# A two-layer transformer prompt kernel: another order of its TensorE products

## The chip, the cores and the metric

The kernel runs on one core of a Trainium2 chip, in one launch. The metric is device microseconds of one execution; of several executions the median is given.

## The reference, cut to what matters

The input is 2048 rows of 576 (one batch). Two blocks are applied twice, with the same weights both times: a block A with residual on its layer norm, and a block B with residual on its layer norm.

```
def _A_ref(x, mem0, Wq, Wk, Wv, Wo, seg_len):      # seg_len 32, 64 segments
    mem = mem0                                      # 8 rows
    for s in range(n_seg):
        h = concat([mem, x[segment s]])             # 40 rows
        q, k, v = h Wq, h Wk, h Wv                  # 32 heads of 128
        p = softmax(mask(q k^T * scale))
        o = (p v) Wo
        mem = o[:, :8]; outs.append(o[:, 8:])
...
x = x + A(layernorm(x)); x = x + B(layernorm(x))
x = x + A(layernorm(x)); x = x + B(layernorm(x))
```

B is a gated FFN, `silu(x w1) * (x w3)` times w2, with 4608 hidden columns. A is recurrent: a segment needs the 8 memory rows that the segment before it put out.

## The kernel before, in words

Work is done in steps t. Step t runs segment t of the first layer and segment t - 8 of the second (LAG 8) side by side: 80 columns where both layers have a segment, 40 where one has. There are 64 + 8 = 72 steps. Every four steps 128 rows of a layer are complete and go through the FFN as a "job"; the FFN weights come from DRAM in 18 pairs of 256 hidden columns for every job, through two buffers for w1 and w3 (tile W13, in the profile W from in_B_w_dram) and two for w2 (W2C). All matmul results go to eight PSUM banks.

The program is a graph of nodes (`make_nodes`): each is a small bundle of instructions on one engine with its cost, the nodes it depends on, and the buffers it takes and gives back. `plan` walks the graph and puts out the order in which the nodes are recorded; each engine then executes its own instructions in that order. For VectorE (DVE), ScalarE (ACT), GpSimd (POOL) and the load queue (SP), `plan` picks the ready node that can start first. For TensorE (PE) the order is fixed beforehand: a string, one letter for each product, `ORDER = FIRST + FOUR * 11 + LAST`. FIRST has 805 letters, FOUR 224 (four steps and their FFN job), LAST 684. The letters that the text uses:

| letter | product | matmuls |
|---|---|---|
| Q, q | queries and keys of one unit of four heads (8 units a step), main part and the last 64 of 576 rows ("tail") | 32, 8 |
| S | scores of a group of 8 heads (4 groups a step) | 16 or 8 |
| T | transposes of the softmax result, written to tile PTS by ACT or DVE | 8 |
| P | T's result times V, copied to tile OT | 8 |
| O, o | OT times Wo, main part and tail | 32, 8 |
| V, v, X, x, G, g | values of the memory rows, of the x rows, or of both, and tails | 8 to 32 |
| F, f | FFN up for one weight pair, main part and tail | 16, 4 |
| W, w | FFN down for two weight pairs, first and second layer | 8 |
| p, n, a, b | transposes around residual and layer norms | 5 |

Between S and T stand seven or eight instructions on DVE and ACT: add of the mask, maximum, subtraction, exp, sum, reciprocal, and three or four multiplications into tile PB. Between F, f and W stand a tanh on ACT and two multiplications on DVE. The first Q of a step needs the memory columns that ACT and DVE write from the last o of the step before.

TensorE works in tile modes. Tails of q, f and g are in "row" mode (two matmuls of 64 rows side by side), o is in "col" mode (64 columns), Q and O are in "full" mode, the narrow V in "c32", "oct" or "quad". T, P, F, W, G, p and n may run in full or in col mode; `plan` lets them take the mode of their neighbours. In col mode `mm` (line 586) splits each matmul into two halves of 64 columns.

All loads of weights are on SP's queue, in the planned order. A load for a buffer waits for the product that reads the buffer's old content. For the last job the weights are not streamed through W13: once the last step has read Wq, Wk and Wv, their tiles W and WV are overwritten by four big loads (`tail_load`, 2.4 MB each for W and 1.2 MB for WV). Pairs 16 and 17 are loaded once for the two last jobs. Every matmul is recorded by line 591, every ACT instruction by 594, DVE 597, SP loads 600, ACT's loads 603.

In step 0 the first Q of units 0 and 4 puts 12 matmuls of 512 columns on the identity ahead of its own (`qk`), if its q has not come before. The X products of step 0 issue nothing of their own; the V of step 0 issues both.

Of the kernel before, what the change touches and what calls it, by code (L numbers as in the profile page):

```python
# [44 lines left out]
class Slot:  # L45


    def __init__(self, pool, users=1):
        self.pool, self.users, self.i, self.end, self.begun = pool, users, None, 0.0, False
# [144 lines left out]
def ewh(*ns):  # L194
# [2 lines left out]


FIRST = (
    "amQQQQqqqqSSqqQQQTSQqqSxXVvPTPTOPOOTooPoOoQQqqqvSVqQQQSqQqqQSTxqPQTSOPXoTOPTaPOOoooQQqqqqQSQQSQqqqVSTvQQqXPTSPTO"  # L200
    "POOToooPOoxQQqqqQSVqvQQqSqQTQPSqqQOTSoPOTPTOPooOoQQpqqqQvSVQnqQFSqfqQQTSfqqFPQFTSOfoPWTOFPfTOPFOoooWQqqfQQSQFfqq"
    "vVfSFTWQFqqfQPQFSqqfQTXPSWTFOfPOTxOPFOooooWQQqqqfQSFqfqVvQWTQSFfqPQQSfqqFTQOSfPFTOaFPWTOPooofOoFQqqfQQSWqqfQFSvV"
    "TQqqQWPQSQTPOqqOboSoTXPXTPOOooxxQQpQqqqVqQnvSSFqfQqQFfQTSfqqFPQTOPSWTFFPffOTOPWOooooFQQqfqqQQqfSWFGSqqgQTQFPQgqf"
    "SGTFqfQOoSPWFfggGTGPOaTWPOOoooFQQvqfqVSFqqfQQQqqfSFQTQFqfqSQWPFfSTOPFTWPOffooOTFPWOooFQqfqqQQWSQQqQqSqqbQSTGggqQ"
    "PGTOSPGTggOPGTOPoooOoQqqqpQpQQqvVSSnnQFqfqqQQTFPqffSQOTWPFOSTwFPffFTOWPwOooooFqqffQQFQqqwWSFqqfQQQwWSTSGqgfFPQFf"
    "qgTGQPGTfgSWFgPGTOOPOOwooooFqqfQQQWQffqqFwFSSVvFQfqqQQTQWqqSwPFaSTffFPOTOWPwfTFPOOooooWQQqqqqQSbQQQSqqGTQgqqSQPG"
    "TgggSGPGTOPOTOPwOoooo"
)
FOUR = (
    "QqqvpQQpQqqVSSnnQQFffqqFQTQqqfSFPwTWFSffOPFTWPOTOPwOooooFqfqqQQQWQqwSSFFffgqGQTQPQgqqqGTwSQPWGSFTfgfgFPGOTOPOwOo"  # L210
    "oooFqffqQFQWQqSVvQQQqqqfFTWPwSSFFqffqQQTOwSWPFTffFOPWTwPOOooooFqqfqQQQWQSqqqaQSQQbQgqqSGTSGPgTGPOTggGPOTOPwOoooo"
)
LAST = (
    "QqqqpQQpQSqqqQQnVvSnSQTFqfqfQPFTOFPoSTwFfPOTOPWOoooFqffqQQQQqqfSFWSGwqqgQQTQPFgqffFTGWwPFSgffqFQWGSwTFPGTgfOPOOO"
    "ooooWFqqfqQQQSwQqqqVSvQTQFPQqSfqfFTQWwPSOTFffPOTOPFOWoooowQQqfqFSQwQWFqqfVSTvWQQqqPQQqqSTOSoPVvwTOPbTOPooxOoXqqQ"
    "QpvQqqSVpQQqqQSTQPqqQSnnOFffToSFPTOPFTOPWOooowQfqfqFQQSvqqVQFSfqqQQwTSWPQFTffqqQOPSWTFPFTOwPOOooooXfqxFQQQqfqfqF"
    "SQwVvSWQFTQqqfqQWPQSTwqffFPOFSWTOPwFffTOPFOWooowoFqqfQQQSFQqfqvVSTQqqfQWwPSFTqqQPQWSTOPOOooowbTxPOoXqqQQQpSQqvqV"
    "qSnQQFffqFQqqSQTPSTFfPOwOToFPofTOPFOoowQfqqfQFSQVvqqqQQSFQfqqqQSQTwPSFTFPffXTOOPxTOPwOooooFQfqqVvQQQSqfqFSQQfqqq"
    "FQTSQPwqOTSFPofTFPOOTPwOoooQfqqqQQSwFQqfqvSVqTQQqPQSQqTSfOPFOTfooPFTOPOooFpwnfffFFwFwfffFFFwfffFFwFwfffFFFwfffFF"
    "wFwfffFFFfww"  # L220
)
ORDER = FIRST + FOUR * 11 + LAST
# [2 lines left out]
class Opt:  # L225

    qk, qkt, sc, tr, pv, wo, wog, vm = 0.0079, -0.0342, 0.0268, 0.1447, 0.0406, 0.2653, 0.0725, 0.1407
    vmt, vx, vxt, ff, fft, win, w2, gstep = -0.0231, 0.2313, 0.0843, 0.2124, -0.1839, 0.8 * (LAG - 4), 0.1943, 0.0624
    ustep, mode_pen, hor, wait, bulk, ff_split, last_win, tail_at = 0.0315, 0.1194, 0.0162, 0.141, 0.02, False, 2.5, -1.5

# [337 lines left out]
class Emitter:  # L568


    def __init__(self, nc, tc, T, aps, nseg):
        self.nc, self.tc, self.T, self.nseg = nc, tc, T, nseg
        self.a = aps
        self.last = {}
        self.order_dep = mybir.DependencyInfo(mybir.DependencyClass.NoSync, mybir.DependencyReason.SCHED_ONLY)
        self.tail_w, self.ys, self.mode = {}, {}, None


    def ch(self, eng, inst):
# [287 lines left out]
    def v_parts(self, strips, r):  # L867

        return [(p0, m, row, 2 * q + r) for p0, _, q, m, row in strips]

    def vx(self, t, k, b, tail):
        def f(n):
            if t == 0 and not tail:
                self.x0 = (b, self.vx_strips(t, k))
                return
            self.v_mm(t, [(b, self.vx_strips(t, k))], tail)
        return f

    def vm(self, t, k, b, tail):
        return lambda n: self.v_mm(t, ([self.x0] if t == 0 and not tail else []) + [(b, self.vm_strips(t, k))], tail)  # L880

    def v_ev(self, b, p0, width, row, blk):
        return lambda n: self.cp(n, self.T.V[row:row + width, blk, :], self.bk(b)[p0:p0 + width, :])
# [444 lines left out]
```

## Time and profile before

| | us |
|---|---|
| median of 4 runs | 2694.91 |
| lowest, highest | 2691.28, 2697.9 |
| the profiled execution | 2697.9 |
| its span | 2696.1 |
| PE busy in it | 2629.5 |
| DVE busy | 2103.5 |
| ACT busy | 1362.0 |

By the starts of the first matmuls in the trace, FIRST begins at 13.3 us and the first FOUR at 530.9; the eleven FOUR take 156.30 to 157.62 us each; LAST begins at 2255.3. A line of a group names the engine, the operation, out<-in with the shapes, the count, the busy time and the mean of one. A line of the timeline has start and length, and in brackets the idle time before and what ended it. "Issue" means that the profile shows nothing that the engine waited for. A busy time of PE is modelled from pipelined matmuls; the distance between starts is the safer measure.

### The profile page before, as it was taken

To read this page: it belongs to the slowest core of one execution; us is meant where nothing else is said; L and a number is where in the kernel's file an instruction comes from. 1 tells how busy PE (TensorE), PEld (TensorE's weight loads), DVE (VectorE), ACT (ScalarE), POOL (GpSimd) and SP (SyncE) were. 2 spreads that over 40 slices of the span, in tenths; PEclk is the share of its full clock that TensorE was granted. 3 is DMA by queue.
4 is the path that set the end of the run, shared out by engine and by line. 5 is a ranking of instruction groups with operands and counts; after the bars stand their busy time and mean duration, and the time that the engine had idled before them with its cause. 6 is when DMAs were issued, how large, how long until landed. Compare 5 with 4: busy or idle time off the path is not lost.

```text
span 2696.1 us, 137075 instructions
## 1 busy us (share of the span) xinstructions
PE 2629.5 (98%) x60995; PEld 2287.0 (85%) x60995; DVE 2103.5 (78%) x5463; ACT 1362.0 (51%) x3938; POOL 332.4 (12%) x400
## 2 busy tenths in 40 slices
PE   5999999999999999999999999999999999999998
PEld 4788888889888888888888888888888888888886
DVE  5777786887888788787878878787887878787776
ACT  2645554554545455454545545454545545454552
POOL 1111110110111011011101101010110101011110
PEclk8999999999999999999999999999999999999999
DMA  9064524343342334334233434424243442434457
GB/s 317 7 179 112 155 83 131 89 128 109 109 128 81 108 96 127 109 111 128 80 111 92 128 108 117 126 80 112 87 128 108 117 126 65 122 89 134 127 169 246
DMA packets 478178, 322.08 MB, mean 119 GB/s; under 512 B 26024, under 2 KB 467760, under 8 KB 476944
## 3 DMA queue, kind: packets, MB, share of 16 engines
q1 hardware_dynamic: 474048, 305.43, 38.6%
q8 instruction: 477, 7.82, 1.2%
q0 software_dynamic: 3024, 6.93, 0.9%
q10 hardware_dynamic: 512, 0.94, 0.1%
q14 instruction: 117, 0.96, 0.1%
HBM read 308.49 MB, written 2.36 MB: 115 GB/s over the span
## 4 chain that ended last, share of the span: by engine, by line
PE 85%; DVE 7%; DMA 3%; ACT 2%; issue 1%; SPq 1%; POOL 0%; ACTq 0%; DVEq 0%
PE bank L591 85%; DVE STAT L597 1%; DMA W<-in_B_w_dram 1%; SPq L600 1%; DVE SME L597 1%; ACT V L594 1%; DVE HTT L597 1%; DVE PB L597 1%; DMA W<-in_A_Wk_dram 1%; DVE V L597 1%; DVE XN L597 0%; DMA WO<-in_A_Wo_dram 0%; DVE LNS L597 0%; DMA XN<-in_A_x_dram 0%; DVE XR L597 0%
## 5 line engine op out<-in xcount | busy, mean ns | idle before, releaser
L591 PEld LDWEIGHTS <-W 128*128 128x128 bf16 (+2 forms) x32176 | 1268.2, 100 | 132.0 <-issue 64.2
L591 PE MATMUL bank<-HT,W 128*128 128x80 bf16 (+3 forms) x23040 | 812.0, 197 | 20.7 <-issue 9.6
L591 PE MATMUL bank<-XTB,W 128*64 128x256 bf16 (+5 forms) x9136 | 660.7, 263 | 7.2 <-DMA W<-in_B_w_dram 4.2
L594 ACT ACTIVATE QKT<-bank 128x64 bf16<-128x64 f32 (+2 forms) x1500 | 349.7, 312 | 352.5 <-PE bank L591 346.8
L1006 POOL MEMSET PB<- 128x1024 bf16 x288 | 274.1, 952 | 1832.4 <-PE bank L591 1553.8
L591 PE MATMUL bank<-OT,WO 128*128 128x80 bf16 (+3 forms) x11520 | 407.0, 198 | 3.3 <-ACT OT L594 1.3
L591 PEld LDWEIGHTS <-WO 128*128 128x128 bf16 (+1 forms) x11520 | 380.0, 102 | 20.7 <-issue 9.2
L594 ACT ACTIVATE V<-bank 64x512 bf16<-64x512 f32 (+1 forms) x606 | 343.0, 585 | 94.6 <-PE bank L591 85.9
L591 PE MATMUL bank<-WV,HT 128*32 128x512 bf16 (+5 forms) x3584 | 373.4, 382 | 1.1 <-DMA WV<-in_A_Wv_dram 0.7
L591 PE MATMUL bank<-W2C,HTT 128*64 128x288 bf16 (+1 forms) x3072 | 323.5, 287 | 0.4 <-DMA W2C<-in_B_w_dram 0.4
L594 ACT ACTIVATE HTT<-bank 128x512 bf16<-128x512 f32 (+1 forms) x324 | 176.6, 553 | 211.3 <-PE bank L591 210.3
L597 DVE TENSOR_REDUCE STAT<-SME 104x8 f32<-104x320 f32 (+1 forms) x576 | 274.2, 476 | 11.5 <-ACT SME L594 6.3
L597 DVE TENSOR_TENSOR PB<-SME,STAT 40x128 bf16<-40x128 f32 (+4 forms) x912 | 275.0, 336 | 8.5 <-DVE STAT L597 0.5
L597 DVE SCALAR_TENSOR_TENSOR XR<-bank,XR 128x288 f32<-128x288 f32 x576 | 245.9, 446 | 23.4 <-PE bank L591 19.2
L597 DVE SCALAR_TENSOR_TENSOR HTT<-HTT,bank 128x512 bf16<-128x512 bf16 (+1 forms) x324 | 201.8, 623 | 74.8 <-ACT HTT L594 70.5
L591 PEld LDWEIGHTS <-HT 128*32 128x32 bf16 (+5 forms) x3584 | 154.4, 98 | 124.5 <-issue 17.0
L591 PEld LDWEIGHTS <-HTT 128*64 128x64 bf16 (+1 forms) x3136 | 223.7, 105 | 34.5 <-issue 1.2
L594 ACT ACTIVATE OT<-bank 128x320 bf16<-128x320 f32 (+1 forms) x420 | 155.2, 403 | 148.9 <-PE bank L591 146.0
L597 DVE TENSOR_TENSOR HTT<-HTT,bank 128x512 bf16<-128x512 bf16 (+1 forms) x324 | 203.7, 629 | 27.8 <-DVE HTT L597 0.5
L594 ACT ACTIVATE SME<-SME 104x320 f32<-104x320 f32 (+1 forms) x288 | 135.3, 470 | 165.9 <-DVE SME L597 164.2
L597 DVE CAST QKT<-bank 128x128 bf16<-128x128 f32 (+4 forms) x548 | 147.6, 316 | 88.6 <-PE bank L591 86.4
L594 ACT ACTIVATE PTS<-bank 128x320 bf16<-128x320 f32 (+1 forms) x383 | 143.9, 403 | 131.8 <-PE bank L591 118.5
(61 smaller groups left out, 1832.6 us busy)
## 6 DMA issues: line engine op xcount, KB each, us to landing
W<-in_B_w_dram SPq DMA_DIRECT2D x612, 256.0 KB, 3.6
W2C<-in_B_w_dram SPq DMA_DIRECT2D x306, 288.0 KB, 3.3
W<-in_B_w_dram SPq DMA_DIRECT2D x612, 32.0 KB, 3.3
W<-in_B_w_dram SPq DMA_DIRECT2D x8, 1024.0 KB, 12.5
W<-in_A_Wq_dram SPq DMA_DIRECT2D x9, 512.0 KB, 9.1
WO<-in_A_Wo_dram SPq DMA_DIRECT2D x4, 1152.0 KB, 17.6
XR<-in_A_x_dram POOLq DMA_DIRECT2D x16, 288.0 KB, 3.7
WV<-in_B_w_dram SPq DMA_DIRECT2D x4, 1152.0 KB, 10.7
```

Of the source, the lines that this page charges most:

```text
L591: self.ch("PE", self.nc.tensor.matmul(out, lhsT=lhsT, rhs=rhs, start=start, stop=stop, skip_group_check=True, **k))
L594: self.ch("ACT", self.nc.scalar.activation(*a, **k))
L597: self.ch("DVE", getattr(self.nc.vector, fn_)(*a, **k))
L600: self.ch("SP", self.nc.sync.dma_start(out=out, in_=in_))
L1006: return lambda n: self.ch("POOL", self.nc.gpsimd.memset(self.T.PB[:, pb.i], 0.0))
```

## The change

The three strings get new contents of the same lengths (805, 224, 684) with the same letters in number. The last 52 letters of LAST, `oFpwnfff...`, are the same. No node, cost, pool or load of the graph is changed. `plan` runs on the new strings, so the orders of DVE, ACT, POOL and SP follow them.

A second edit lets the V and the X of step 0 stand in either order: the one that comes second issues the matmuls of both, where before it was always V.

```diff
 FIRST = (
-    "amQQQQqqqqSSqqQQQTSQqqSxXVvPTPTOPOOTooPoOoQQqqqvSVqQQQSqQqqQSTxqPQTSOPXoTOPTaPOOoooQQqqqqQSQQSQqqqVSTvQQqXPTSPTO"
+    "amqqQQQqSQqqQqSqqQSQTSvxVXPTPTOPTOPooOOooQQqqqqQSQvqqSVQqQTqSQPQOSToPXTOPTxoPOOooQqqqQQSVvqQQSQqqqSqTQPQOSTPTOP"
...
 FOUR = (
-    "QqqvpQQpQqqVSSnnQQFffqqFQTQqqfSFPwTWFSffOPFTWPOTOPwOooooFqfqqQQQWQqwSSFFffgqGQTQPQgqqqGTwSQPWGSFTfgfgFPGOTOPOwOo"
-    "oooFqffqQFQWQqSVvQQQqqqfFTWPwSSFFqffqQQTOwSWPFTffFOPWTwPOOooooFqqfqQQQWQSqqqaQSQQbQgqqSGTSGPgTGPOTggGPOTOPwOoooo"
+    "QvqqpQQpQqqVSSnnQQFqfqfFQTQfqqWSFPwTFPSfOOTFPwTOPWOooooFffqqQQQQqqSWFSFffqgGQTQPQQgqqqGSwTFPGSfgfgFTGOPOWTOPwOoo"
+    "ooFqqQQQQqfqVvSSwWFfqfqQQTFWQwQSFffqqFPWTOPSowTFPffOTOFPWwOoooFqqfqQQQWQSqqqaQSQQbQqgqSGTSGPgTGPOTggOPGTOPwOoooo"
 )
...
-    "FQTSQPwqOTSFPofTFPOOTPwOoooQfqqqQQSwFQqfqvSVqTQQqPQSQqTSfOPFOTfooPFTOPOooFpwnfffFFwFwfffFFFwfffFFwFwfffFFFwfffFF"
+    "QQPwqqFTSOfPFTOfPwTOPfoooOoFQQqqqqQSQQSqqQVvSfTFPqQQwqfTSFPOTOFPTOPfoooOoFpwnfffFFwFwfffFFFwfffFFwFwfffFFFwfffFF"
     "wFwfffFFFfww"
...
+    def v_run(self, t, b, strips, tail):
+
+        if t or tail:
+            self.v_mm(t, [(b, strips)], tail)
+            return
+        self.v0.append((b, strips))
+        if len(self.v0) == 2:
+            self.v_mm(t, self.v0, False)
+
     def vx(self, t, k, b, tail):
-        def f(n):
-            if t == 0 and not tail:
-                self.x0 = (b, self.vx_strips(t, k))
-                return
-            self.v_mm(t, [(b, self.vx_strips(t, k))], tail)
-        return f
+        return lambda n: self.v_run(t, b, self.vx_strips(t, k), tail)
```

More of the change, by code (lines that the diff above doesn't have):

```diff
@@ L199 @@
 FIRST = (
-    "amQQQQqqqqSSqqQQQTSQqqSxXVvPTPTOPOOTooPoOoQQqqqvSVqQQQSqQqqQSTxqPQTSOPXoTOPTaPOOoooQQqqqqQSQQSQqqqVSTvQQqXPTSPTO"
[L201 to L204, printed above, removed]
@@ L205 @@
-    "PGTOSPGTggOPGTOPoooOoQqqqpQpQQqvVSSnnQFqfqqQQTFPqffSQOTWPFOSTwFPffFTOWPwOooooFqqffQQFQqqwWSFqqfQQQwWSTSGqgfFPQFf"
-    "qgTGQPGTfgSWFgPGTOOPOOwooooFqqfQQQWQffqqFwFSSVvFQfqqQQTQWqqSwPFaSTffFPOTOWPwfTFPOOooooWQQqqqqQSbQQQSqqGTQgqqSQPG"
-    "TgggSGPGTOPOTOPwOoooo"
+    "amqqQQQQqSQqqQqSqqQSQTSvxVXPTPTOPTOPooOOooQQqqqqQSQvqqSVQQqTqSQPQOSToPXTOPTxoPOOooQqqqQQSVvqQQSQqqqQSqTQPOSTPTOP"
+    "OToooPaOoQQqqqqQQSvSVQqqqQQQSqTPSXTOPTOPoTxoPOOooQQpQqqqvVqSnQQSFfqFQqfqqQTQSPFTfSOFPWOToPFToffPOOooWQqqqqQQSQQS"
@@ new lines @@
+    "FFfqfVvqTQWQqSFxffqQFPSXTWfPFTOPOTOPFOooooWQfqqqQQSFqfqVvQQSFfqTQPWQSqqfFTQOSfoPFTOPWFTOPooffOoFQqqQqqvSQQWSVqqf"
+    "FQQWqqSTQPQSTOPabOTXPooTOPxxOooXqqpQQQqqSQnVvfSFTQqqqQQPSFffqQFTOPoSWTFfPOOTFPWOooofQQqfqqFSQFqqfgQGWTQPQSfqFQQq"
+    "fqFSWTGFSggfGPGTOPOTfgFaPOOooooWVvqqfQQFFQSqfqQWQSqqfFQTQQqfqSFPWTSFPOTfoOPFWTOPffFOoooWQQqqqqQSbQQQqgqSGSTGPQTq"
+    "gqQPOggSGTGPOTOPoooOoQqqqpQVpSQnQvqqqQnQFSTffqFQQPqSwTFPSffOOWTFPFTOPWOoooowFffqqQQQWSfqqFQwQSFqfqgGTQQPWfqSTFFg"
+    "gfqGQwPGTOoSPFgfOGTOPWOoooFqqfqQQQQvSwqVSFqqfQQWwTFPQfqfqFTQSwPWSfFOTFPWwOTffFPOOaooooWQQqqqqQwSbQGQgqqSQTQPQqqg"
@@ L208 @@
+    "SGTSGPGggTOPOTOPoooOo"
 )
 FOUR = (
-    "QqqvpQQpQqqVSSnnQQFffqqFQTQqqfSFPwTWFSffOPFTWPOTOPwOooooFqfqqQQQWQqwSSFFffgqGQTQPQgqqqGTwSQPWGSFTfgfgFPGOTOPOwOo"
-    "oooFqffqQFQWQqSVvQQQqqqfFTWPwSSFFqffqQQTOwSWPFTffFOPWTwPOOooooFqqfqQQQWQSqqqaQSQQbQgqqSGTSGPgTGPOTggGPOTOPwOoooo"
+    "QvqqpQQpQqqVSSnnQQFqfqfFQTQfqqWSFPwTFPSfOOTFPwTOPWOooooFffqqQQQQqqSWFSFffqgGQTQPQQgqqqGSwTFPGSfgfgFTGOPOWTOPwOoo"
+    "ooFqqQQQQqfqVvSSwWFfqfqQQTFWQwQSFffqqFPWTOPSowTFPffOTOFPWwOoooFqqfqQQQWQSqqqaQSQQbQqgqSGTSGPgTGPOTggOPGTOPwOoooo"
@@ L212 @@
 )
 LAST = (
[L214 to L218, printed above, removed]
@@ L219 @@
-    "FQTSQPwqOTSFPofTFPOOTPwOoooQfqqqQQSwFQqfqvSVqTQQqPQSQqTSfOPFOTfooPFTOPOooFpwnfffFFwFwfffFFFwfffFFwFwfffFFFwfffFF"
+    "QqqqpQQQSnpQQqqqVSvTSnQFffqPFOQqTwPoSWTFPffFTOOWPwOoooFFqfqQQQqqfSQQwQfqqFTSGSqfgQFPWQgfqGTSFPGFTfggOOPGTOPwWOoo"
+    "ooFFqffqQQwQWQSqqVSvqqQQTFQPSfqqQwTOWSPFTFPofOTOPwOoooWFfqfqQQQQqfqSFwWvVSFTfqqQQPWQqqSvTQVSPOTbOPwOTooPoxOoXqQp"
+    "pVvQqqqQSQQnqqSQnqQFTSfqQPFTSOPfTFOPwTOPWOooooFqfqfQQQSVqqqvQQQwSfqFWTFPSfqqQTQOPSFTwfFPOTOPWOooooFfqqQQQSqfxvVX"
+    "qfFQwWTSQFQqqqfQPWSTwFPffqQFTWSOwFPffOFTOPwOooooWFvqfqQQQSWqqVQwSFfqqfQFTQQSqqWPQTPSOoTOPwOToobPxOoXqqqQQQpvSVqQ"
@@ L220 @@
+    "qQSnqQFfSTQFPqqfQOTSFfPwTOoofPFTOPFOfoowQqqQFSQfqqqQQSVvqqfQFTQFSfqPQOTowPSFTfxXPOTOPFOooowVvqqQQQSqqfQQSqqfQFST"
+    "QQPwqqFTSOfPFTOfPwTOPfoooOoFQQqqqqQSQQSqqQVvSfTFPqQQwqfTSFPOTOFPTOPfoooOoFpwnfffFFwFwfffFFFwfffFFwFwfffFFFwfffFF"
     "wFwfffFFFfww"
@@ L575, in __init__ @@
         self.order_dep = mybir.DependencyInfo(mybir.DependencyClass.NoSync, mybir.DependencyReason.SCHED_ONLY)
-        self.tail_w, self.ys, self.mode = {}, {}, None
+        self.tail_w, self.ys, self.mode, self.v0 = {}, {}, None, []
     def ch(self, eng, inst):
@@ L869, in v_parts @@
         return [(p0, m, row, 2 * q + r) for p0, _, q, m, row in strips]
-    def vx(self, t, k, b, tail):
-        def f(n):
-            if t == 0 and not tail:
-                self.x0 = (b, self.vx_strips(t, k))
-                return
-            self.v_mm(t, [(b, self.vx_strips(t, k))], tail)
-        return f
+    def v_run(self, t, b, strips, tail):
[5 more added lines that the diff above has]
+            self.v_mm(t, self.v0, False)
+    def vx(self, t, k, b, tail):
+        return lambda n: self.v_run(t, b, self.vx_strips(t, k), tail)
     def vm(self, t, k, b, tail):
-        return lambda n: self.v_mm(t, ([self.x0] if t == 0 and not tail else []) + [(b, self.vm_strips(t, k))], tail)
+        return lambda n: self.v_run(t, b, self.vm_strips(t, k), tail)
     def v_ev(self, b, p0, width, row, blk):
```

## The prediction

> **What bounds the kernel now.** I read the page from its first block down: busy shares, the slices, the chain that ended last, then the loads.
>
> ```profile
> span 2696.1 us, 137075 instructions
> PE 2629.5 (98%) x60995; PEld 2287.0 (85%) x60995; DVE 2103.5 (78%) x5463; ACT 1362.0 (51%) x3938; POOL 332.4 (12%) x400
> ...
> PEclk8999999999999999999999999999999999999999
> ...
> q8 instruction: 477, 7.82, 1.2%
> ...
> PE 85%; DVE 7%; DMA 3%; ACT 2%; issue 1%; SPq 1%; POOL 0%; ACTq 0%; DVEq 0%
> ...
> W<-in_B_w_dram SPq DMA_DIRECT2D x612, 256.0 KB, 3.6
> ```
>
> PE is busy 98% of the span and is 85% of the chain. Is a busy PE also a fast PE? The windows view by stage answers (stretch, length, PE busy, PEld, DVE, ACT, POOL, clock, DMA share, GB/s); the stages are the head, the rest of FIRST, the eleven repeats of FOUR, LAST, and the last FFN.
>
> ```profile
> 0.00:60.00 60.00, 31.88 (x772) 24.12 (x774) 28.53 (x72) 14.23 (x39) 10.34 (x23) 0.89 1.02 350
> 60.00:531.00 471.00, 457.95 (x11723) 394.83 (x11715) 367.39 (x986) 255.06 (x772) 64.93 (x74) 0.99 0.38 108
> 531.00:2255.00 1724.00, 1717.35 (x38368) 1505.54 (x38367) 1370.83 (x3542) 883.50 (x2518) 203.74 (x242) 1.00 0.38 109
> 2255.00:2650.00 395.00, 385.33 (x9570) 331.97 (x9570) 308.41 (x793) 199.85 (x587) 52.31 (x60) 0.99 0.45 131
> 2650.00:2696.00 46.00, 36.97 (x582) 30.55 (x579) 28.29 (x71) 9.39 (x24) 1.13 (x2) 1.00 0.75 252
> ```
>
> The head is bound by loads (DMA share 1.02), the middle by PE at full clock, the end partly by loads again. For the middle I took the start of each matmul in the trace's timeline, in the order of the letters, so each letter has a time from its first matmul to the next letter's first.
>
> ```profile
> 1317.19 2.46 PE L591 MATMUL bank<-HT,W 128*128 128x80 bf16 x64
> 1319.48 0.45 PE L591 MATMUL bank<-ident,YTS 128*128 128x128 bf16 x5
> ...
> 1329.01 0.45 PE L591 MATMUL bank<-HT,W 64*128 64x80 bf16 x16
> 1329.39 1.92 PE L591 MATMUL bank<-XTB,W 128*128 128x256 bf16 x16
> ```
>
> Two Q start at 1317.19 and the next product at 1319.48: 2.29 us for 64 matmuls, 36 ns each for 80 columns, so the stream is dense. Two q in row mode take 0.38 us to the next product, though a q followed by a q takes 0.144: 2 x 0.144 = 0.29, and the last 0.095 is the change of tile mode. Medians over the whole trace: row to full 95 ns (244 cases), full to row 95 (218), full to col 93 (143), col to full 118 (86), col to row 135 (140). One repeat of FOUR is then 149.24 us of products, 57 changes of mode for 5.93 us, and 1.1 us of lateness in the cleanest repeat (156.30 us). The eleven together take 1724.42 us, 5.2 us over eleven clean ones. So the order of the letters can win only changes of mode and waits; the products stay.
>
> **The change part by part.** The sum is made against the profiled execution's own 2697.9 us (span 2696.1 and 1.8 around it), the highest of four; their median is 2694.91, 3.0 lower.
>
> *Products.* The same 3953 letters are issued. The changed kernel's PE row count is 60925 pairs against 60995: fewer of the flexible products fall into col mode, where each matmul is split in two. That split costs no time: P takes 285 ns in col and 286 in full, T 286 and 288, F 1732 and 1757. Taken at 0, bounds +-0.5 us.
>
> *Changes of mode.* Counted in the planned orders: FIRST 275 to 272, FOUR 57 to 55, LAST 208 to 215. Priced by kind: -0.23, 11 x -0.205 = -2.25, and +0.77 us. **-1.7 us.** This is the surest term.
>
> *Waits in FOUR.* The waits view of 531 to 2255 us shows what PE stood still for:
>
> ```profile
> PE bank L591 <- ACT HT L594: 3.8, 11, 0.3
> PE bank L591 <- DMA W<-in_B_w_dram: 1.6, 4, 0.6
> ```
>
> The first is the end of a step: the last o, then Q of the next step, which needs the memory columns. It is 0.39 us late once a repeat; the new FOUR also has one such pair directly adjacent, so it stays. The second is weights. W13 has two buffers, so load n+2 is issued when product n lets go; the products between set how much time it has, against 3.6 us from issue to landing plus its issue. In the old FOUR three of eighteen loads have under 5.5 us (4.8, 4.9, 5.3), and at the 4.9 one, 39 letters in, f waits in five of the eleven repeats. In the new FOUR one has (4.9), the next 6.7. I take 1.3 of the 5.2 us as gone, since not all of it is weights. Bounds: -5.2 (all gone) to +5.4 (one new wait of 0.49 a repeat, the price of a P directly after its T below). On SP's queue the loads move with the products; for no load does an earlier one in the queue, waiting for its own buffer, take time from it, in either order.
>
> *LAST.* Letters that directly follow what they need: P after its own T (PTS must be copied; 0.49 us late), O after its own P (0.43), Q after the last o (0.34 with one layer). Old LAST has 2, 2 and 2 (one of the last at FOUR's price), new LAST 1, 0 and 1: 0.49 + 0.86 + 0.34 = **-1.7 us.** The scores chain, S to its T, is 4.9 us at the shortest in old LAST with both layers and 5.4 in the new. Bounds -5 to +3.
>
> *The last loads.* SP issues in order, and this is where LAST is decided:
>
> ```profile
> 2636.59 0.54 SPq L600 DMA_DIRECT2D WV<-in_B_w_dram  x1
> 2645.73 5.35 SPq L600 DMA_DIRECT2D W<-in_B_w_dram  x8
> ```
>
> From 2637.1 to 2645.7 SP holds: next in its queue is the weight pair 17, which needs the buffer that F of pair 15 reads until then, and the three big last loads are queued behind it. Between, the DMA share falls to nothing; after it the queues run at some 390 GB/s to 2682, and PE waits for what lands:
>
> ```profile
> 2673.27 0.40 PE L591 MATMUL bank<-XTB,W 64*128 64x128 bf16 x8
> 2674.80 0.23 PE L591 MATMUL bank<-XTB,W 64*128 64x128 bf16 x1 [1.13 <-DMA W<-in_B_w_dram]
> ...
> 2682.42 0.39 PE L591 MATMUL bank<-XTB,W 128*128 128x128 bf16 x4
> 2683.95 0.84 PE L591 MATMUL bank<-XTB,W 128*128 128x128 bf16 x12 [1.15 <-DMA W<-in_B_w_dram]
> ```
>
> In the new order F of pair 15 stands before P1 and O0 of the last step instead of behind them. These are 0.21 + 0.80 = 1.0 us, so the loads start 1.0 us earlier against the same end. **-1.0 us**; bounds 0 to -2.7, all that f and F wait here (1.29 + 0.18 + 1.3). The last 52 letters are the same.
>
> *Head.* FIRST now begins with the tails qq, so the 12 warm-up matmuls ahead of unit 0 (18.05 to 22.7 us) go; 12 ahead of unit 4 appear instead. Q waits for Wk either way. The cover is the loads: the last piece of WO lands at 55.4 us (a chain entry of 11.9 us from 43.5), the last O of step 0 needs it in both orders, and SP's queue is unchanged through all attention weights. Without the cover, the last 3 of unit 4's warm-up matmuls, behind the last of Wk at 33.4 us, cost 3 x 0.21 to 0.44 = 0.6 to 1.3 us. V's loads land at 43.4 and PE idles there; taken at 0. Rest of FIRST: adjacent P after T 4 to 3, Q after o 4 to 5, O after P 2 and 2: **-0.2 us**, bounds -5 to +5.
>
> [...]
>
> *Instruction fetch.* PE stands still for 1 to 3 us in the middle of a product with nothing to wait for: at matmuls 3415 and 3543, and at 60016 and 60144, each pair 128 matmuls or 256 instructions apart, as one of the 477 packets of 16 KB holds. Ten such stops make some 14 us, nearly all in FIRST and LAST. They fall where a packet meets a burst of loads, so a new order reshuffles them. Taken at 0, bounds -6 to +6.
>
> Sum: -1.7 - 1.3 - 1.7 - 1.0 - 0.2 = -5.9. Own time 2697.9 - 5.9 = 2692.0; from the median **2689.0 us**.
>
> **The rivals.**
>
> *Nothing moves.* The waits that go are replaced by others one product further on, or the time is given back in fetch stops. For it: DVE is 78% busy, so results come late in bunches. Only modes are left, -1.7, and a little fetch: 2694.
>
> *More goes.* All 5.2 us of FOUR's extra and half of the fetch stops: 2694.9 - 1.7 - 5.2 - 1.7 - 1.0 - 4 = 2681. For it: the tight weight loads fall from three to one in FOUR and, under 5.5 us, from nine to five in LAST.
>
> *Slower.* FOUR repeats one new stall eleven times. Its place: letter 164, a T that comes 5.2 us of products behind its S, where the old FOUR's shortest is 6.2; and letter 151, a W2 2.9 us behind its F, where the old has 4.1. The S to T chain by its rows is 0.48 + 0.48 + 0.49 + 0.47 + 0.48 + 0.20 + 3 or 4 x 0.34 = 3.6 to 4.0 us and its hops; in LAST, T came 5.65 and 5.77 us behind S where products filled 5.05 and 5.42. That would be 0.5 us here, and a W2 that needs the 3.8 us once measured in FIRST 0.9 more; with a part of the second, 1.0 a repeat: 2694.9 - 4.6 + 11 = 2701. It decides from 0.9 us a repeat. Against it: old FIRST ran such W2 at 3.2 us unhindered, and old LAST a T at 4.9.
>
> **How the numbers follow.** Forecast 0.40, more goes 0.20, nothing moves 0.23, slower 0.17. 0.2%, about what a measurement of this kernel can tell from no change, is 5.4 us: under 2689.5 is faster, over 2700.3 slower. The forecast lies on that border and gives 0.27 of its 0.40 to faster: with 0.20, 0.47. The rest, 0.13 + 0.23, is same: 0.36; slower 0.17. Range 2680 to 2701: 2681 and 2701 are the outer cases, and the open bounds (fetch, FOUR's waits) reach past both.
>
> **What would show it.** FOUR's repeats at about 156.1 us when clean, nearer each other than now; if they stand at 156.8 or more with T or W2 late, the slower case. No wait of f 39 letters into FOUR. F of pair 15 done and SP free about 1 us earlier against the end, and shorter waits for W in the last 25 us. The end of step 0, near 57 us, unchanged. Wrong I would be if fetch stops differ by over 5 us in sum, or a product waits for a bank, which no row of the trace names.

## The result, and the profile after

The changed kernel takes 2688.23 us (median of 41 runs, 2682.43 to 2696.24), the kernel before 2693.77 us beside it (62 runs, 2689.84 to 2700.59). The ratio is 0.9979, 95% interval [0.9975, 0.9983]: 5.7 us less, with an interval of 4.6 to 6.7. The profiled execution took 2684.33 us, its span is 2682.6. That of before took 2697.9, so the two profiles differ by 13.6 us, more than twice what the medians do.

The head of the page of the changed kernel, and the line of the chain by engine:

```profile
span 2682.6 us, 136879 instructions
...
PE 2622.9 (98%) x60925; PEld 2290.2 (85%) x60925; DVE 2113.1 (79%) x5486; ACT 1346.5 (50%) x3915; POOL 332.2 (12%) x400
...
PE 89%; DVE 3%; ACT 3%; DMA 2%; issue 1%; SPq 1%; POOL 0%; ACTq 0%; DVEq 0%; POOLq 0%
```

PE's share of the chain went from 85% to 89%, DVE's from 7% to 3%. PE waits less for DVE. The windows of the changed kernel by stage, with the columns as before:

```profile
0.00:60.00 60.00, 30.57 (x639) 21.14 (x640) 28.69 (x70) 13.64 (x35) 10.34 (x23) 0.83 1.00 347
...
530.00:2250.00 1720.00, 1714.74 (x38192) 1511.17 (x38192) 1376.71 (x3553) 871.00 (x2508) 202.89 (x241) 1.00 0.38 108
2250.00:2640.00 390.00, 385.01 (x9712) 332.38 (x9713) 303.37 (x783) 203.28 (x599) 52.56 (x60) 1.00 0.46 135
2640.00:2682.50 42.50, 34.73 (x527) 29.16 (x522) 27.83 (x69) 9.01 (x23) 1.13 (x2) 0.97 0.74 249
```

The middle and the end are shorter, but the head is not: in the first 60 us PE has done 639 matmuls where it had done 772, at a clock of 0.83 where it was 0.89. The record of the clock starts at 24.1 us before and at 24.7 us after, and the view counts what lies ahead as full clock. That is not so: the 12 warm-up matmuls of before took 0.42 us each from 18.05 us on, as long as those of the changed kernel from 29.8 us on, where the granted clock was 0.50.

One execution is not enough here, because single stops of 1 to 3 us come and go between executions. The next table takes all profiled executions of this study that have the old or the new string in a stage, from letter to letter by the first weight load of each product. Kernels that alter something else in the stage are left out of its row. The number is the mean of the executions; in brackets are their range and their count.

| stage | old string | new string | difference | predicted |
|---|---|---|---|---|
| step 0, first matmul to first Q of step 1 | 43.7 (43.2 to 44.2, 6) | 47.3 (46.8 to 47.7, 3) | +3.6 | 0 |
| rest of FIRST | 468.4 (465.6 to 473.9, 6) | 466.6 (464.1 to 468.6, 7) | -1.8 | -0.2, modes -0.2 |
| eleven FOUR | 1723.1 (1722.3 to 1724.4, 5) | 1720.1 (1719.9 to 1720.4, 7) | -2.9 | -1.3, modes -2.25 |
| LAST with the last FFN | 440.8 (438.5 to 442.7, 5) | 436.0 (432.9 to 438.7, 6) | -4.8 | -2.7, modes +0.8 |
| sum | | | -5.9 | -5.9 |

So the sum came out at what was forecast, but not by the forecast's terms: a loss of 3.6 us in the head that was not forecast stands against a gain of 4.8 us in LAST where 1.9 were forecast. With means of three to seven executions, and ranges of up to 8 us, that the sum meets the measured 5.7 us so closely is chance.

What PE waited for in LAST up to the last FFN, by the waits view (total us, times, longest), before:

```profile
PE bank L591 <- issue: 3.1, 3, 1.8
PE bank L591 <- ACT HT L594: 1.0, 3, 0.4
PE bank L591 <- ACT QKT L594: 1.0, 3, 0.4
PE bank L591 <- DVE V L597: 0.9, 1, 0.9
PE bank L591 <- ACT OT L594: 0.8, 2, 0.5
PE bank L591 <- DVE PB L597: 0.8, 2, 0.5
PE bank L591 <- ACT PTS L594: 0.7, 2, 0.4
...
```

and in the changed kernel:

```profile
PE bank L591 <- issue: 3.3, 4, 1.6
PE bank L591 <- ACT HT L594: 0.3, 1, 0.3
PE bank L591 <- ACT PTS L594: 0.3, 1, 0.3
...
```

Left out before are XR 0.6, ACT's XTB 0.4 and DVE's QKT 0.2 us, and after ACT's XTB and DVE's HT, 0.3 us each. Without the lines "issue", 16 waits of 6.4 us became 4 waits of 1.2 us. "Issue", the stops in the middle of a product, is as long as before.

Not all of LAST's gain need be waits. Up to the last FFN (from its first product, the `n` of `oFpwn`, to the end) LAST takes 398.8 us in the five old executions and 393.8 in the six new ones; the last FFN itself takes 42.1 and 42.2. In the stretch up to the last FFN the granted clock is half for 6.8 to 10.2 us in the old executions (6.8 in the kernel before) and for 0 to 5.5 in the new (0 in the changed kernel). By the distance of the matmuls' starts there, against the same matmuls at full clock, that is an estimated 1.7 us lost in the mean of the old and 0.8 in that of the new. So some 0.8 of the 4.8 us goes with the clock; whether the order brings that was not tested.

In FOUR the view of the changed kernel names nothing but the end of a step:

```profile
PE bank L591 <- ACT HT L594: 3.8, 11, 0.3
```

The line with the weights (1.6 us in four waits) is gone; ten of the eleven repeats take 156.26 to 156.38 us, the other 156.48.

### The profile page after: what moved, and what is told of

It reads as the page before. It is cut to its first block, busy times and chain, and to the rows that moved or that the text cites. A ratio compares the mean times of both kernels' runs of the same rounds, so it can differ in the third digit from the quotient of the medians.

```text
span 2682.6 us, 136879 instructions
## 1 busy us (share of the span) xinstructions
PE 2622.9 (98%) x60925; PEld 2290.2 (85%) x60925; DVE 2113.1 (79%) x5486; ACT 1346.5 (50%) x3915; POOL 332.2 (12%) x400
## 4 chain that ended last, share of the span: by engine, by line
PE 89%; DVE 3%; ACT 3%; DMA 2%; issue 1%; SPq 1%; POOL 0%; ACTq 0%; DVEq 0%; POOLq 0%
PE bank L591 89%; ACT V L594 2%; DMA W<-in_B_w_dram 1%; SPq L600 1%; DVE STAT L597 1%; DVE V L597 1%; DMA W<-in_A_Wk_dram 1%; DVE SME L597 1%; DVE HTT L597 0%; DVE PB L597 0%; DMA XN<-in_A_x_dram 0%; ACT SME L594 0%; DVE PTS L597 0%; ACT PTS L594 0%; ACT QKT L594 0%
## 5 line engine op out<-in xcount | busy, mean ns | idle before, releaser
L594 ACT ACTIVATE QKT<-bank 128x256 bf16<-128x256 f32 (+2 forms) x1477 | 343.6, 314 | 363.1 <-PE bank L591 335.0
L594 ACT ACTIVATE V<-bank 32x512 bf16<-32x512 f32 (+1 forms) x594 | 335.8, 585 | 110.2 <-PE bank L591 103.9
L591 PE MATMUL bank<-WV,HT 128*32 128x512 bf16 (+4 forms) x3680 | 375.9, 385 | 0.3 <-DVE HT L597 0.3
L591 PEld LDWEIGHTS <-HT 128*32 128x32 bf16 (+4 forms) x3680 | 158.1, 100 | 119.8 <-issue 17.8
L591 PEld LDWEIGHTS <-HTT 128*64 128x64 bf16 (+1 forms) x3104 | 229.5, 104 | 32.1 <-DVE HTT L597 0.4
L597 DVE CAST QKT<-bank 128x128 bf16<-128x128 f32 (+4 forms) x571 | 154.7, 317 | 122.4 <-PE bank L591 121.4
L597 DVE SCALAR_TENSOR_TENSOR XR<-bank,XR 128x288 f32<-128x288 f32 x576 | 239.5, 446 | 13.7 <-PE bank L591 11.0
```

The costliest lines, as they stand in the source:

```text
L591: self.ch("PE", self.nc.tensor.matmul(out, lhsT=lhsT, rhs=rhs, start=start, stop=stop, skip_group_check=True, **k))
L594: self.ch("ACT", self.nc.scalar.activation(*a, **k))
L597: self.ch("DVE", getattr(self.nc.vector, fn_)(*a, **k))
```

## The experiments

Every ratio is to the kernel before, timed on the same chip, with its 95% interval. The medians of the kernel before were 2688.9 to 2690.2 us there. A start of step 1 in this part is that of its first matmul, 0.4 us behind the first weight load by which the table goes.

### The parts, each alone

The change is three strings, so each can be put in alone: the new FOUR with the old FIRST and LAST (only_four), the new LAST (only_last), the new FIRST (only_first), and all three new but for the first 42 letters, which are step 0 (new_oldhead).

In the kernels the strings themselves are replaced; written as sums, the four orders are as follows. Kernels with the old head carry the change's second edit too, which alters nothing in the old order.

```diff
-ORDER = FIRST + FOUR * 11 + LAST
+ORDER = OLD_FIRST + NEW_FOUR * 11 + OLD_LAST          # only_four
+ORDER = OLD_FIRST + OLD_FOUR * 11 + NEW_LAST          # only_last
+ORDER = NEW_FIRST + OLD_FOUR * 11 + OLD_LAST          # only_first
+ORDER = OLD_FIRST[:42] + NEW_FIRST[42:] + NEW_FOUR * 11 + NEW_LAST   # new_oldhead
```

> Only FOUR has its new order; FIRST and LAST are the old ones. Theory 1 (the weight waits that vary from repeat to repeat are a steady loss of the old order, and go): 3.5 to 4.5 us below the kernel before, every repeat within 0.2 us of 156.36 in the trace, no wait for W in the eleven repeats. Rival (what the profiled execution of before showed above its cleanest repeat was chance, and the new clean repeat of 156.36 is no shorter than the old 156.30): within 1 us of the kernel before.

Measured: 2683.52 us, ratio 0.9979 [0.997, 0.9988], 5.6 us less. The trace shows 1720.2 us for the eleven FOUR and no wait for weights. The table's 2.9 us lie just below the interval, which is 3.2 to 8.1 us, so some of this gain is not seen in FOUR's length. One repeat of the eleven took 156.61 us, the others 156.26 to 156.37.

> Only LAST has its new order. Theory 1 (fewer products directly behind what they need, and the last loads released about 1 us earlier against the end): 2 to 3.5 us below the kernel before, LAST and the last FFN together nearer 436 than 441 us. Rival (the 8 us that the two profiles differ by in LAST and after it are all of the change's gain): 5.5 to 8 us below.

Measured: 2684.43 us, ratio 0.9985 [0.9976, 0.9994], 4.0 us less, with an interval of 1.6 to 6.5 that holds the theory and touches the rival. The trace doesn't bear the theory out in full: LAST with the last FFN takes 438.7 us, not nearer 436 than 441. LAST up to the last FFN is short (393.5 us), but the last FFN takes 45.2, with 3.3 us of waits for W and 9.0 us at half clock.

> Only FIRST has its new order. Theory 1 (the new step 0 ends 4.4 us later than the old and the rest of FIRST wins it back): within 1.5 us of the kernel before; in the trace step 1 begins near 61 us instead of 57. Rival (the late step 0 was chance of one execution): step 1 begins near 57 us, 3 to 5 us below the kernel before.

Measured: 2691.06 us, ratio 1.0013 [1.0004, 1.0022], 3.5 us **more**, which neither the theory nor the rival had. The first Q of step 1 starts at 60.03 us, as the theory has it; that the rest of FIRST wins this back doesn't show in the time. The three parts add up to -0.21 - 0.15 + 0.13 = -0.23%, the whole to -0.21%. Each has an interval of about 0.09% to either side, so within that they don't work on each other.

> The changed kernel with the first 42 letters of FIRST (all of step 0) in the old order. Theory 1 (the new step 0 costs 4.4 us because V's 64 matmuls run at half clock there and all of the rest waits for them): 3 to 4.5 us below the changed kernel, so 8.5 to 10 us below the kernel before, and V of step 0 done near 44.4 us instead of 49.3. Rival (what is won in step 0 is given back further on, at the loads): equal to the changed kernel.

Measured: 2681.94 us, ratio 0.9974 [0.9965, 0.9983]; step 1 starts at 57.71 us, 44.6 us after the first matmul. So the trace has the head's loss in the first 42 letters. The time bears it out in part: 7.0 us below the kernel before (4.6 to 9.4) where 8.5 to 10 were expected, and by the ratios only 1.3 us below the changed kernel, with intervals that overlap.

### The head: clock or order?

The timeline of PE in step 0, before:

```profile
39.58 3.11 PE L591 MATMUL bank<-WV,HT 64*32 64x512 bf16 x56
43.41 1.39 PE L591 MATMUL bank<-WV,HT 128*32 128x512 bf16 x24 [0.72 <-DMA WV<-in_A_Wv_dram]
```

and in the changed kernel:

```profile
29.77 5.27 PE L591 MATMUL bank<-W,ident 128*128 128x512 bf16 x12 [3.42 <-DMA W<-in_A_Wk_dram]
34.84 2.39 PE L591 MATMUL bank<-HT,W 128*128 128x40 bf16 x88
...
42.77 6.97 PE L591 MATMUL bank<-WV,HT 64*32 64x512 bf16 x80
```

The 12 warm-up matmuls came at 18 us, ahead of unit 0, and ran while PE waited for the keys' weights. In the new order they belong to unit 4, wait 3.4 us for its weights, and then hold its products back to 34.84 us; the last of those weights landed at 33.4 in the kernel before. And the 80 matmuls of V and X take 7.0 us in one piece where they took 3.1 and 1.4: they ran at half clock. The windows view from 42 to 48 us has it (the third number from the end is the clock), first before, then the changed kernel:

```profile
42.00:48.00 6.00, 2.73 (x56) 1.22 (x45) 4.56 (x9) 4.51 (x8) 0.00 (x0) 1.00 1.07 386
```

```profile
42.00:48.00 6.00, 5.63 (x65) 2.15 (x68) 4.59 (x14) 1.34 (x5) 0.94 (x1) 0.50 1.08 386
```

Further kernels are to tell late products and half clock apart.

after_warmq: the changed kernel, its warm-up reads the queries' weights of unit 4, which land earlier.

```diff
-self.mm(..., self.T.W[:, 4 + c, u * 512:(u + 1) * 512], True, True)
+self.mm(..., self.T.W[:, (c if u else 4 + c), u * 512:(u + 1) * 512], True, True)
```

> The changed kernel with one word altered in the head: the 12 warm-up matmuls ahead of unit 4 read the queries' weights, which have landed, instead of the keys', whose last pieces land until 33.4 us. So they run in the gap of 3.4 us ahead of them and not behind it. Theory (the new head loses 4.4 us by half clock: the gap of 26.3 to 29.8 us and the late warm-up leave V and X of step 0 at half clock, 7.0 us for what takes 4.5): unit 4's products start at about 33.4 instead of 34.8, V and X run at full clock for most of their length, the first Q of step 1 starts at 57 to 58.5 us instead of 61.4, ratio to the kernel before 0.9965 to 0.997 against 0.9979 of the changed kernel. Rival (the new order of the head is what is late, S and V behind other letters; the clock matters little): only the 1.4 us of the late warm-up go at most, step 1 starts at 60 us or later, ratio 0.9975 to 0.998.

Measured: 2681.47 us, ratio 0.997 [0.9958, 0.9981]. The warm-up now starts at 25.60 us, in the gap, and V and X take 4.2 us:

```profile
40.67 4.19 PE L591 MATMUL bank<-WV,HT 64*32 64x512 bf16 x80
```

Step 1 starts at 57.15 us with the new order of letters: that is 44.7 us after the first matmul, and the old order takes 43.6 to 44.6, so the order itself is hardly late. But the cure doesn't hold in every execution: the last kernel of this study (best_w2pool) has the same head, and its V and X took 6.57 us at half clock:

```profile
41.58 6.57 PE L592 MATMUL bank<-WV,HT 64*32 64x512 bf16 x80
```

That sizes the two causes, by one execution each: step 1 starts 48.1 us after the first matmul in the changed kernel, 46.6 with the early warm-up and half clock in V, and 44.7 with the early warm-up and full clock. About 1.5 us go with the late warm-up and about 2 with the clock.

after_again is the changed kernel once more, after_nowarm the same without any warm-up matmuls, old_nowarm the kernel before without them.

```diff
-for c in range(4 if first and t == 0 and u % 4 == 0 else 0):
+for c in range(0):
```

> The changed kernel itself once more, on the same chip as the two others of this call. Theory (the head costs 4 us and the rest of the change wins 9 to 10): step 1 starts 47 to 48 us after the first matmul, ratio 0.9975 to 0.9983; LAST and the last FFN together 433 to 438 us. Rival (what the trace of the changed kernel shows of the head is a single draw): step 1 starts about 44 us after the first matmul as in the old order.

Measured: 2683.89 us, ratio 0.998 [0.9971, 0.9988]; step 1 starts 47.1 us after the first matmul. So the late head is not one draw; V and X took 6.46 us.

> The changed kernel without the 12 warm-up matmuls ahead of unit 4 (there are none ahead of unit 0 in its order), so the order is the new one and nothing runs in the gap or behind it. Theory 1 (half clock in V and X of step 0 is what costs, and the gap ahead of unit 4 brings it): unit 4's products start 1.3 us earlier than in the changed kernel, but V and X still take 6 to 7 us for 80 matmuls, step 1 starts about 46 to 47 us after the first matmul, 1 to 1.5 less than in the changed kernel, ratio 0.997 to 0.9978. Theory 2 (the late warm-up is the whole of it): step 1 starts at about 44 us as with the warm-up in the gap, ratio 0.9965 to 0.997. Rival (the warm-up is worth its time even behind the gap): step 1 later than in the changed kernel, over 48 us, ratio 0.998 or more.

Measured: 2687.44 us, ratio 0.9988 [0.9978, 0.9997]. The trace is nearly as theory 1 has it: unit 4's products have their last weights at 33.46 us, V and X take 5.88 us (6 to 7 were expected), step 1 starts 46.9 us after the first matmul. The time is longer than it expected; the profiled execution has a stop of 3.0 us on "issue" in LAST, but whether that explains eleven runs stays open.

> The kernel before without the 12 warm-up matmuls ahead of unit 0; its order is the old one. [...] Theory (covered in the old order: O of step 0 waits for WO in any case, and V for its loads): step 1 starts within 1 us of the old 43.2 to 44.2 us after the first matmul, ratio 0.9995 to 1.0005. Rival (half clock moves to V as in the new order): step 1 starts 2 to 4 us later, ratio 1.0008 to 1.0015.

Measured: 2691.93 us, ratio 1.0007 [0.9998, 1.0016], which can't be told from none by the times. The trace tells it: V and X take 6.81 us, and step 1 starts 46.9 us after the first matmul where it started at 43.7:

```profile
41.31 6.81 PE L591 MATMUL bank<-WV,HT 64*32 64x512 bf16 x80
```

That is the rival, in one execution, and there the theory of the cover falls: in the old order too the missing warm-up is worth 3 us, and the loads of WO don't hide it. Not all of it is V: measured from the first matmul, V starts 2.2 us later than in the kernel before, and takes 6.8 us where it took 5.2 with its wait for WV. The granted clock was half from 29.5 to 46.5 us. From 42 to 48 us it was 1.00 in the kernel before and in after_warmq, 0.50 in the changed kernel, 0.62 in old_nowarm and in best_w2pool.

### The weights in FOUR

old_fswap: the kernel before, with an O put between F and f at the place where f waits.

```diff
-    "...SFPwTWFSffOPFTWPO..."
+    "...SFPwTWFSOffPFTWPO..."
```

> The kernel before, with one exchange in FOUR: letters 37 to 40 read SOff instead of SffO, so an O (1.07 us) stands between the F whose end frees the W13 buffer and the f that needs the next load. It costs one more change of tile mode a repeat (11 x about 0.1 = 1.1 us). Theory (FOUR's gain is the weight wait 39 letters in, and nothing else of the new order): the waits of f on W in FOUR go (1.6 us in 4 waits before), the repeats lie within 0.3 us of each other at about 156.4, FOUR as a whole takes 1720.5 to 1722 against 1722.3 to 1724.4 with the old string, ratio about 0.9992 to 0.9997. Rival (the waits come from the bursts of loads as a whole and move to the next tight load, the ones at 4.8 and 5.3 us): FOUR stays at 1722.3 to 1724.4 plus 1.1, ratio 1.0000 to 1.0005.

Measured: 2691.31 us, ratio 1.001 [1.0001, 1.0019]; the eleven FOUR take 1724.6 us. The waits view over its eleven FOUR names the end of a step as before, no weights, and two new lines:

```profile
PE bank L591 <- issue: 3.5, 22, 0.2
PE bank L591 <- DVE HTT L597: 2.0, 11, 0.2
```

The line "issue" is a gap in the record: 64 of the 60995 matmuls have no row in this trace, five of them in each repeat, and old_noload below has the same 22 stops in repeats that are no longer for it. The wait for weights is gone, as the theory said; in its place a W a few letters on waits in each repeat for HTT, the product of DVE that comes out of the f which now stands later. That, and one more change of mode, cost more than the four waits. The theory was right on the wait and wrong on the time; the rival had the sign, from another wait than it named.

old_noload: the kernel before, with the streamed loads of w1 and w3 left out after the second pair.

```diff
 def load_w13(self, pr, w13):
     def f(n):
+        self.loads13 = getattr(self, "loads13", 0) + 1
+        if self.loads13 > 2:
+            return
```

> The kernel before without the streamed loads of w1 and w3: only the first two weight pairs are loaded, every later F and f reads what lies in the two buffers, so the FFN is computed from the wrong weights. All products, the loads of w2 and the big loads for the last FFN stay. Theory A (all that FOUR loses over eleven clean repeats is waits for these loads): the eleven repeats take 156.3 us each within 0.15, FOUR 1719.5 to 1720, that is 3 to 4.5 us less. Theory B (the stops of instruction fetch in the middle of a product come where a packet of instructions meets a burst of weight loads): the steady stops near matmuls 2522, 3543, 5075 in FIRST and 51274 in LAST, 1.2 to 3 us each, go, and FIRST and LAST shorten by some 5 us together. Rival to B (a stop belongs to a place in the program and not to the loads): they stay at the same matmuls at the same size, FIRST and LAST shorten by under 1 us.

Measured: 2680.11 us, ratio 0.9967 [0.9955, 0.9979]. The old FOUR takes 1720.4 us, its repeats 156.29 to 156.59, a little over theory A's 1719.5 to 1720: that is the new FOUR's length, with none of its letters. So all that the new FOUR wins goes with the streamed loads. That it is waits for them shows by the letters: in the kernel before, the eleven repeats take 4.2 us more than eleven of the 156.38 us that is the median repeat here, and 2.7 of them stand at the two f of letters 38 and 39 (counted from 0) and 0.8 at the q and f of letters 28 and 29. For "issue" in the rest of FIRST (60 us to the first FOUR), first the kernel before, then this one:

```profile
PE bank L591 <- issue: 7.0, 8, 2.9
```

```profile
PE bank L591 <- issue: 0.3, 2, 0.2
```

The stops at matmuls 3543 and 5075 are gone and the rest of FIRST takes 461.4 us where it took 465.6 to 473.9: theory B. Two of the four places that the expectation names were no such stops. At 2522 and 51274 PE waits for DVE (PB, and the write-out of V from a bank), at the same size with and without loads. In the last step, where the big loads run, three stops stay, 4.6 us in all and the longest 2.8.

### The last loads

old_f15: the kernel before, F of pair 15 ahead of O0 and P1, which is the one step that the prediction priced.

```diff
-    "...QSQqTSfOPFOTfooPFTOPOooFpwn..."
+    "...QSQqTSfFOPOTfooPFTOPOooFpwn..."
```

> The kernel before, with one letter of LAST moved: in the last step F of weight pair 15 stands ahead of O0 and P1 (SfFOPOT) instead of behind them (SfOPFOT). FIRST and FOUR are the old ones. Theory (the last loads decide the end): SP's queue comes free about 1.0 us earlier, the three big last loads start and land 1.0 us earlier, the waits for W in the last FFN shrink by as much, the whole is 1.0 us shorter (ratio 0.9996, at the edge of what five rounds can tell; the trace must show it: the last eight pieces of W issued about 1.0 us earlier against the start of LAST). Rival (the loads are not what ends last; the products of the last step are only rearranged): the loads start earlier, PE's last FFN starts at the same distance from LAST's start, no change, ratio 1.0000. Second rival (O0 behind F makes the last o late): LAST grows by up to 1.7 us.

Measured: 2688.75 us, ratio 0.9996 [0.9987, 1.0005]. The last FFN waits 0.5 us for W where the other old ones wait 1.2 to 3.2, but LAST with the last FFN takes 440.4 us against 440.8: the stops on "issue" in the same stretch (5.2 us here, 2.9 to 5.0 in the others) vary by more than the effect. Inconclusive on the gain; the changed kernel shows a reason why it didn't get it. SP's queue there:

```profile
2633.24 5.43 SPq L600 DMA_DIRECT2D W<-in_B_w_dram  x8
2641.89 0.89 SPq L600 DMA_DIRECT2D W2C<-in_B_w_dram  x2
...
2654.18 8.40 SPq L600 DMA_DIRECT2D W<-in_B_w_dram  x4
```

The x8 is what F of pair 15 releases. It goes out 8.5 us ahead of the last FFN's first product where it was 7.9 before, so the release is earlier, by 0.7 us. Behind it SP holds again: W2C goes out at 2641.89, 0.1 us after the w ahead of the last FFN is through and the last FFN's first product starts (2641.76), and the big loads stand behind it. In the kernel before it is the same 0.1 us (2653.70 after 2653.58). So best_w2pool takes that hold away: the changed kernel with the warm-up in the gap, and these two loads on GpSimd's queue.

```diff
-lds.append(node("DMA", ..., em.load_w2(pr_, w2), prio=prio - 0.99, acq=[w2], ...))
+lds.append(node("SWD" if keep else "DMA", ..., em.load_w2(pr_, w2, keep), deps=last_w2[-1:] if keep else [], ...))
...
-return lambda n: self.dma(self.T.W2C[:, w2.i], ...)
+return lambda n: (self.swdma if keep else self.dma)(self.T.W2C[:, w2.i], ...)
```

> The changed kernel with the warm-up in the gap (as in after_warmq) and the two last loads of W2C (pairs 16 and 17) on GpSimd's queue instead of SP's. In every kernel so far SP holds once more after the last eight pieces of W: the next in its queue is W2C, whose buffer the first w of the last FFN reads, and the last big loads of WV and W stand behind it; they go out 0.1 us after the first product of the last FFN, whatever the release before it. Theory (that hold, and not F of pair 15, decides the wait for the last W): SP goes on at once, the last four pieces of W are issued 4 to 6 us earlier against the start of the last FFN, F's wait of 2.0 to 2.5 us goes, the last FFN takes 38 to 40 us instead of 40.7 to 42.7; ratio to the kernel before 0.9955 to 0.9968. Rival (the transfer itself is the limit: the three big loads need their 37 us at full rate in any case): F's wait stays over 1.5 us, ratio as after_warmq, 0.997. Second rival (W2C comes late on GpSimd's queue, which also holds the power of the layer norm): the first w waits 1 us or more in its place.

Measured: 2681.77 us, ratio 0.997 [0.9958, 0.9981], no better than after_warmq. SP, and the waits of its last FFN:

```profile
2627.87 5.45 SPq L601 DMA_DIRECT2D W<-in_B_w_dram  x8
...
2647.80 8.99 SPq L601 DMA_DIRECT2D W<-in_B_w_dram  x4
```

```profile
PE bank L592 <- DMA W2C<-in_B_w_dram: 1.6, 2, 0.8
PE bank L592 <- DMA W<-in_B_w_dram: 0.8, 1, 0.8
```

WV follows the x8 at once (2633.36), so SP doesn't hold any more, yet the last four pieces go out 11.4 us after the last FFN's first product, only 1 us earlier than in the changed kernel (12.4), not 4 to 6. F's wait falls to 0.8 us and W2C costs 1.6 in its place: that is the second rival. The first has the time right, but F's wait, which it put over 1.5 us, wrong. From the issue of the x8 to the F that waits for the last W it is 37.5 us here (2665.40), 37.4 in the changed kernel (2670.59), 38.2 before (2683.95), so the transfer may be what is left. But over all executions it is 37.0 to 41.2, and the two of 41.2 (after_nowarm, after_warmq) have the x8 out 12 us ahead of the last FFN, not 8.5, and F's wait as long as ever, 2.0 and 2.4 us: there the second hold decides. Which of the two limits stands in the changed kernel stays open.

## Why the prediction was right, and where it was wrong

The total was right: 5.9 us forecast, 5.7 measured. That is luck in good part, since of the terms only the waits in FOUR and the neighbours in LAST came as described, and two misses of some 3 us, the head's and LAST's, stand against each other. By its own steps:

- **Products, 0.** Nothing in the traces speaks against it.
- **Changes of mode, -1.7, "the surest term".** Not seen as time. The biggest part was 0.205 us for each FOUR, but a repeat takes 156.37 us in the new order (the median; the cleanest 156.26), and without the loads the old order has 156.38 (the cleanest 156.29). By the prediction's prices the new one has 5.72 us of modes instead of 5.93, and so 1.40 us of lateness at 156.36 instead of 1.13 at 156.30. Where that comes from shows by the letters: to the next product, the W at letter 104 takes 1.11 us and the W at letter 30 takes 1.00, where others take about 0.9. The forecast of some 156.1 us failed.
- **Waits in FOUR, -1.3.** Right in kind and too small. All of FOUR's -2.9 us is this term; without loads the old FOUR is as short. The caution "not all of it is weights" was wrong. The slower rival's places, T at letter 164 and W2 at 151, were not late.
- **LAST, -1.7.** Mis-sized. The prediction counted letters that directly follow what they need. These did what it said: PTS, OT and ACT's HT fell from 0.7 + 0.8 + 1.0 to 0.3 + 0 + 0.3 us, -1.9. Of the rest, QKT 1.2, V 0.9, PB 0.8, XR 0.6 and XTB 0.1 us went and 0.3 for DVE's HT came, another -3.3 that was not counted. That is the two profiles; some 0.8 us of the gain in the means goes with the clock. V is a bank that DVE was still emptying; "a product waits for a bank, which no row of the trace names" was wrong, since this row of before names one: f of LAST stops until DVE's cast of V is done.

```profile
2272.80 0.38 PE L591 MATMUL bank<-XTB,W 64*128 64x256 bf16 x3 [0.89 <-DVE V L597]
```

- **Last loads, -1.0.** Nothing won. The x8 does go out 0.7 us earlier, but the step "so the loads start 1.0 us earlier against the same end" failed for the big loads behind it: SP's second hold, on W2C, which the prediction doesn't have, and some 37 us of transfer stand in between. F's and f's waits for W are 2.5 us before and 2.5 after, and the last FFN takes 42.1 us in the old executions and 42.2 in the new.
- **Head, 0.** Failed, +3.6 us. "The cover is the loads" is the wrong step: V's matmuls are not behind WO, they come first, and O, P and the last o follow them one after the other. What delays V reaches the end of step 0 nearly whole: V and X end 4.9 us later in the changed kernel's profile, step 1 starts 4.5 us later. The parts are the warm-up behind the gap, which the prediction did price (0.6 to 1.3 us without the cover), and half clock in V, which it didn't have.
- **Rest of FIRST, -0.2.** The table has -1.8, but the old executions alone spread by 8 us, so this stays open.
- **Instruction fetch, 0.** Right as a sum: over the whole span "issue" is 11.7 us before and 10.0 after, and the stops in the rest of FIRST are 1.6 to 7.0 us in the old orders and 2.8 to 5.1 in the new. That they come with bursts of loads was right for the rest of FIRST: 7.0 us before, 0.3 without the streamed loads.

The granted clock counts for more in the head than the forecast gave it. In the kernel before it is half at 30.9 to 37.7, 48.0 to 54.8, 119.6 to 126.5, 157.2 to 160.6 and 215.2 to 218.6 us, up to the first FOUR: the starts lie 5, 26, 37 and 54 times 3.41 us behind the first, and the lengths are 3.4 and 6.8. In the changed kernel it is half at 28.1 to 34.9, 41.7 to 48.5, 52.0 to 58.8 and 99.8 to 103.2 us: 4, 7 and 21 times 3.41 us behind the first, with the same two lengths. The grid lies elsewhere in the two: the record of the clock, which is on it, starts at 24.1 us in the one and at 24.7 in the other. That its place is why the same head was at full clock in V in after_warmq and at half in best_w2pool is the author's guess; no run shows it. Ahead of V both were at half clock for a step of the grid, from 35.2 and from 36.3 us, in which PE was busy for 3.22 of 3.40 us; full clock followed in the one and half in the other. In the traces of the two kernels, up to the first FOUR, half clock ended after steps in which PE was busy 0.93 to 1.00 of the time and went on after 0.33 to 0.91; the pair above did both at 0.95. So no run here shows a threshold.

## What to carry to other kernels

Count waits from the waits view, line by line, and ask of each whether the new order still has it, instead of looking only for neighbours in the order: results two or three products away, and banks still being emptied, were two thirds of the waits that LAST lost. A wait that is taken away is worth its length only if the next thing is ready: one letter moved in FOUR took the weights' wait and gave it back at W, and a load moved off SP's queue took 1.6 us of wait for W and gave 1.6 us back at W2C. Where a stretch waits for loads, look at which engine's work comes last behind them before calling a loss covered, and keep filler work inside the gap, not behind it.

## What was not expected of the hardware

- Half clock came for stretches of 3.4 us or multiples (up to 17.1 us in old_nowarm) that start on a grid of 3.41 us. Its place differs between the two kernels' executions: the record starts at 24.1 us before and at 24.7 after. Twelve matmuls more or less at 18 to 23 us went with the clock some 20 us later: V and X took 3.11 and 1.39 us in the old head with them (the same in the kernel before, only_four and new_oldhead; the granted clock from 42 to 48 us was 1.00 before), and 6.81 us in the one without (0.62).
- PE's stops in the middle of a product, with nothing that the profile shows to wait for, need the weight loads in the rest of FIRST: 1.6 to 7.0 us in six executions of the old order, 0.3 us in the one without the streamed loads. At given places of the program (matmuls 3543 and 5075) they come in most executions of the old order: 2.9 and 1.5 us in the kernel before, and the longest stop there is 1.0 to 2.9 us in the six. The five longest of them in the kernel before, at matmuls 3415, 3543, 4181, 4819 and 5075, lie multiples of 128 matmuls apart, to within two. The page has 60995 rows of PE, as many of PEld and 477 packets in the instruction queue: by the author's estimate 255.7 instructions a packet if they are PE's alone, so 128 matmuls. That instruction fetch is what stops PE is inferred from this, not shown.
